# An attention-then-experts kernel: the hand-written order of all engines renewed, and the last branch laid out anew with prefetch hints

## The chip, the cores and the metric

The kernel runs on one core of one Trainium2 chip. The metric is device microseconds of one execution, and the median over several runs. The core's engines are named as in the profile: PE is TensorE (matmuls), PEld its weight loads, DVE is VectorE, ACT is ScalarE, POOL is GpSimd and SP is SyncE. A "q" behind a name (PEldq, SPq) means the instructions that the engine's sequencer handles itself: waits, branches, register loads, DMA issues.

## The reference, cut to what matters

An attention with 32 memory slots per head runs first; its output, 4608 tokens of 512 numbers, goes through a dense pair of matrices and through one of eight experts, chosen per token:

```python
a = softmax(phi, axis=2)                      # over the sequence
k_m = einsum('bhsm,bhsd->bhmd', a, k); v_m = einsum('bhsm,bhsd->bhmd', a, v)
attn_out = softmax(q @ k_m.T / sqrt(64)) @ v_m                 # 8 batches, 8 heads, 576 x 64
x = attn_out.transpose(0, 2, 1, 3).reshape(4608, 512)
y = maximum(x @ w1_dense, 0) @ w2_dense
e = argmax(x @ w_gate, axis=1); g = softmax(x @ w_gate)[e]
y += g * (maximum(x @ w1[e], 0) @ w2[e])                       # per token its own expert
```

## The kernel before

The eight batches are worked one after the other, overlapped by about a batch. For batch b the steps are, in the order of their data: loads `Lphi`, `Lk`, `Lv`, `Lq`; the exponential of phi (`e0`, `e1`, ACT); its column sums (`z`) and the sums with k and v (`kv`, both PE); scaling (`rz`, `kvm`, DVE); turning (`T`, PE) and copying (`kTc`, `vTc`); turning q (`qT0`, `qT1`, DVE); scores (`s`, PE), exponential (`ET0`, `ET1`, ACT), sums (`Z0`, `Z1`, PE), logarithm and inverse (`ln`, `inv`, ACT), the product `A0`, `A1` (DVE). The values are not multiplied out: they are folded into the first matrix of each expert (`fd` dense, `fe` chosen expert; PE), copied (`vd`, `ve`), and the hidden rows are made from A (`hd0..3`, `he0..3`, PE, each 8 matmuls), made non-negative (`Hd`, `He`, ACT or DVE) and multiplied by the second matrix (`yd0..4`, `ye0..4`, PE, each 4 matmuls of 128x512, the last of 64 rows). `Yd` writes the dense part of the output tile `y` (ACT or DVE), `Ye` adds the expert's part (DVE).

One expert is guessed for a whole batch (`choose`, DVE, from the mean value; `wv` reads the number into a POOL register) and its two matrices are loaded (`w1`, `w2`, POOL's queue), or copied from an earlier batch's slot (`cw1`, `cw2`, DVE). For each token `gates` finds the true expert. `pn` (PE) and `flags` (DVE, five small instructions) count the tokens whose expert was another. If there are any, a block with the slow way (`others`, one body per batch, 8 bodies of some 950 PE instructions) runs; with this data there are none, and every engine but SP reads the count from memory, branches past the block and goes to the closing barrier.

The order of everything is written out by hand: the table `ORDER` names each step with its batch and, after a slash, its engine (A for ACT, V for DVE, P for POOL) or, for `warm`, the number of dummy matmuls. Each engine executes its own steps in that order. Loads of q, k, v and the matrices are issued by POOL, the stores `o0`, `o1` (512 KB each) and `o4` (two of 64 KB) by SP, each queue in the order of the table.

Three things around the change are needed below. The output tile `y` has four buffers (`NKEEP`), so the fifth batch's first `Yd` waits until all stores of one earlier batch have landed, and which batch that is follows from the order of the stores. The dense and the expert part of a row share three accumulators of PSUM (the pool `one`), so a `Yd` that waits keeps an accumulator. And the last batch (7) folds its gate into the hidden rows, so that its `Yd` step stands behind `ye`.

## Time and profile before

| | us |
|---|---|
| median of 3 runs | 169.8 (169.19 to 170.12) |
| the profiled execution | 169.38 |
| its span, first to last instruction | 167.7 |
| TensorE busy | 149.8 (89% of the span) |
| VectorE busy | 119.9 (72%) |
| ScalarE busy | 94.0 (56%) |
[...]

The profile's times count from the span's first instruction. 169.38 less 167.7 leaves 1.68 us outside the span. "Idle before" and "waits" name the instruction that waited, how long its engine stood still, and who ended the wait.

### The profile page before, as it was taken

The numbers are of one execution on the slowest core, as the hardware profiler recorded it, in microseconds if no ns is written. First come the engines' busy times: TensorE is split into PE (matmuls) and PEld (weight loads), VectorE is DVE, ScalarE is ACT, GpSimd is POOL, SyncE is SP. The second block draws the span as 40 slices with busy tenths as digits, with TensorE's granted clock in tenths as the row PEclk, the third lists the DMA queues.
The fourth block names the chain that finished last, engine by engine and source line by source line (L and its number), as shares of the span: only waits on it lengthen the run. The fifth ranks groups of instructions, "written<-read, shape, count | busy, mean of one in ns | idle before, by whom it ended". The sixth has DMA issues, their size and how long they took to land.

```text
span 167.7 us, 4923 instructions
## 1 busy us (share of the span) xinstructions
PE 149.8 (89%) x2011; PEld 83.5 (50%) x2011; DVE 119.9 (72%) x354; ACT 94.0 (56%) x190; POOL 33.8 (20%) x56
## 2 busy tenths in 40 slices
PE   7969999999988999999999977699999999999900
PEld 2334455455555664565465633354554765655300
DVE  0524566787997999999598861979788997985110
ACT  3200564695539758964996388228289979630210
POOL 7810251009000750090002002940000000000000
PEclk9999999999999999999999999999999999999995
DMA  5999999999999999999999998999999299831460
GB/s 138 152 203 228 257 211 213 210 257 232 210 260 230 214 265 212 206 254 234 211 225 245 162 277 350 138 192 208 279 207 212 66 349 381 306 119 58 156 260 8
DMA packets 20500, 36.04 MB, mean 215 GB/s; under 512 B 1268, under 2 KB 14580, under 8 KB 20472
## 3 DMA queue, kind: packets, MB, share of 16 engines
q0 software_dynamic: 16336, 25.63, 79.7%
q1 hardware_dynamic: 4056, 9.98, 16.2%
q8 instruction: 17, 0.28, 0.6%
q14 instruction: 11, 0.09, 0.2%
q10 hardware_dynamic: 80, 0.07, 0.2%
HBM read 51.92 MB, written 9.44 MB: 366 GB/s over the span
## 4 chain that ended last, share of the span: by engine, by line
PE 39%; DMA 31%; DVE 14%; issue 5%; ACT 3%; POOL 1%; POOLq 1%; SPq 1%; DVEq 1%; ACTq 0%
PE p_y L788 20%; DMA kv<-in_v_dram 16%; PE p_h L712 10%; DMA W<-in_moe_w_dram 8%; DMA out_dram<-y 6%; DVE y L830 3%; PE p_kv L370 2%; PE p_vw L693 2%; DVE W L606 2%; PE p_x L320 1%; PE p_s L454 1%; ACT ET L467 1%; DVE qT L438 1%; DVE A L515 1%; POOLq L585 1%
## 5 line engine op out<-in xcount | busy, mean ns | idle before, releaser
L788 PE MATMUL p_y<-w2d,HTd 128*128 128x512 f16 (+1 forms) x192 | 37.3, 346 | 2.6 <-DVE y L823 2.3
L788 PE MATMUL p_y<-W,HTe 128*128 128x512 f16 (+1 forms) x192 | 36.0, 346 | 0.4 <-ACT y L821 0.4
L752 ACT ACTIVATE HTd<-p_h 128x576 f16<-128x576 f32 x27 | 16.8, 650 | 18.4 <-PE p_h L712 18.3
L830 DVE SCALAR_TENSOR_TENSOR y<-p_y,gm,y 128x512 f32<-128x512 f32 (+1 forms) x35 | 23.6, 692 | 3.9 <-PE p_y L788 2.2
L788 PEld LDWEIGHTS <-HTd 128*128 128x128 f16 (+1 forms) x192 | 14.6, 101 | 15.7 <-issue 4.8
L788 PEld LDWEIGHTS <-HTe 128*128 128x128 f16 (+1 forms) x192 | 14.8, 101 | 15.3 <-issue 4.1
L240 POOL DMA_DIRECT2D W<-in_moe_w_dram x8 | 4.6, 570 | 87.5 <-DMA W<-in_moe_w_dram 30.5
L821 ACT ACTIVATE y<-p_y 128x512 f32<-128x512 f32 (+1 forms) x25 | 14.0, 567 | 12.4 <-PE p_y L788 12.3
L320 PE MATMUL p_x<-onesb 128*128 128x512 f16 x68 | 19.0, 422 | 1.2 <-DVE ones L258 1.2
L712 PE MATMUL p_h<-A,vwd 128*128 128x288 f16 x128 | 19.6, 286 | 0.3 <-DVE A L515 0.2
L712 PE MATMUL p_h<-A,vwe 128*128 128x288 f16 x128 | 19.2, 286 | 0.0
L467 ACT ACTIVATE ET<-p_s 128x512 f16<-128x512 f32 x16 | 9.7, 604 | 12.6 <-PE p_s L454 12.6
L823 DVE TENSOR_SCALAR y<-p_y 128x512 f32<-128x512 f32 (+1 forms) x15 | 9.3, 632 | 8.3 <-PE p_y L788 4.5
L752 ACT ACTIVATE HTe<-p_h 128x576 f16<-128x576 f32 x21 | 13.2, 659 | 3.5 <-PE p_h L712 3.5
L332 ACT ACTIVATE E<-phi 128x576 f16<-128x576 f32 x16 | 10.6, 681 | 7.6 <-DMA phi<-in_phi_dram 7.6
L712 PEld LDWEIGHTS <-vwd 128*128 128x128 f16 x128 | 11.7, 97 | 6.2 <-issue 1.6
L712 PEld LDWEIGHTS <-vwe 128*128 128x128 f16 x128 | 11.8, 98 | 5.7 <-issue 0.8
L392 DVE TENSOR_SCALAR kvm<-p_kv,rz 128x64 f16<-128x64 f32 (+1 forms) x32 | 8.0, 310 | 6.0 <-PE p_kv L370 5.7
L515 DVE TENSOR_TENSOR A<-ET,lnz 128x576 f16<-128x576 f16 x16 | 11.5, 750 | 1.1 <-ACT lnz L508 1.0
L438 DVE STREAM_TRANSPOSE qT<-q 128x512 f32<-128x512 f32 x16 | 11.0, 691 | 0.2 <-DMA q<-in_q_dram 0.2
L320 PEld LDWEIGHTS <-onesb 128*128 128x128 f16 x68 | 6.6, 106 | 9.2 <-issue 3.4
L508 ACT ACTIVATE lnz<-lnz 128x576 f32<-128x576 f32 x16 | 10.7, 690 | 0.2
(95 smaller groups left out, 195.9 us busy)
## 6 DMA issues: line engine op xcount, KB each, us to landing
W<-in_moe_w_dram POOLq DMA_DIRECT2D x16, 512.0 KB, 8.6
out_dram<-y SPq DMA_DIRECT2D x16, 512.0 KB, 5.2
kv<-in_v_dram POOLq DMA_DIRECT2D x8, 576.0 KB, 17.6
kv<-in_k_dram POOLq DMA_DIRECT2D x8, 576.0 KB, 15.7
q<-in_q_dram POOLq DMA_DIRECT2D x8, 576.0 KB, 15.5
phi<-in_phi_dram POOLq DMA_DIRECT2D x7, 576.0 KB, 16.4
out_dram<-y SPq DMA_DIRECT2D x15, 64.0 KB, 4.9
phi<-in_phi_dram SPq DMA_DIRECT2D x2, 288.0 KB, 4.2
```

The costliest lines, as they stand in the source:

```text
L320: nc.tensor.matmul(p_x, lhsT=onesb, rhs=onesb[:, 0:1].to_broadcast([128, 512]), start=True, stop=True)
L332: nc.scalar.activation(out=x["E"][:, :, hs].rearrange("p t j m -> p j t m"), in_=x["phi"][:, hs], func=AF.Exp,)
L438: nc.vector.transpose(out=o[:, :, 0 : 2 * KQ], in_=i[:, 0:n].rearrange("p (h t) d -> p h t d", h=NP))
L467: nc.scalar.activation(out=ET.rearrange("m (h c) -> m h c", h=2)[:, :, 0:256].rearrange("m h (p k) -> m h p k", k=KQ), in_=p_s[:, :, 0:256 ...
L508: nc.scalar.activation(out=lnz, in_=lnz, func=AF.Exp, scale=-1.0)
L515: eng.tensor_mul(out=st[b]["A"][:, a], in0=st[b]["ET"][:, a, 0:S], in1=st[b]["lnz"][:, a])
L712: nc.tensor.matmul(p_h[:, h, 0:HC], lhsT=vw[:, g, 128 * ft : 128 * ft + 128], rhs=a[:, g, HC * h : HC * h + HC], start=(g == 0), stop=(g = ...
L752: nc.scalar.activation(out=o, in_=in_[:, :, 0:HC], func=AF.Relu)
L788: nc.tensor.matmul(p_y[n * u : n * u + n, to : to + w], lhsT=HT[:, ft, at], rhs=w2[:, ft, w * u : w * u + w], start=(first and ft == 0), s ...
L821: nc.scalar.activation(out=o, in_=p_y, func=AF.Copy, scale=1.0 / SC)
L823: nc.vector.tensor_scalar(out=o, in0=p_y, scalar1=1.0 / SC, scalar2=None, op0=ALU.mult)
L830: nc.vector.scalar_tensor_tensor(out=o, in0=p_y, scalar=x["gm"][:, c : c + 1], in1=o, op0=ALU.mult, op1=ALU.add)
```

## The change

The table `ORDER` is replaced by another one with the same steps (66 dummy matmuls in place of 68, the step `nap` gone, a step `hint` new; some copies go to ACT in place of DVE and the other way round). The planner that writes such a table now has the waits for output buffers in its model. The last branch gets a label, its block is laid out right behind the branch instruction (it falls through into the block when the count is not zero, and jumps when it is zero), and a prefetch hint for this branch is put on PE, DVE, ACT and POOL.

```diff
 ORDER = """
-Lphi1:0 cones:0 Lwg:0 cid:0 warm:0/4 Lphi0:0 Lv:0 warm:0/4 Lk:0 Lq:0 e0:0 Lw1d:0 warm:0/4 e1:0 Lphi:1/P
+Lphi0:0 cones:0 Lwg:0 Lv:0 cblk:0 warm:0/4 Lphi1:0 cid:0 warm:0/4 Lk:0 e0:0 Lq:0 e1:0 Lphi:1/P warm:0/1
...
-ye4:7 ye3:7 Yd4:7/V o4:7/A yd1:7 Yd3:7/A yd0:7 o0:6 ye1:7 ye0:7 Yd1:7/V ye2:7 Yd0:7/A o0:7 pn:0 Yd2:7/A
-flags:0 o1:7 nap:7
+he2:7 He1:7/V yd2:7 He2:7/A ye4:7 ye3:7 Yd4:7/A o4:7/A yd1:7 Yd3:7/A yd0:7 o0:0 ye1:7 ye0:7 Yd1:7/A pn:0
+ye2:7 Yd0:7/A flags:0 o0:7 Yd2:7/V o1:7
...
+    @step("hint")
+    def _(b, i, e):
+        tc.mark_branch_hint_location("fix", engines=(ENG.PE, ENG.DVE, ENG.Activation, ENG.Pool))
...
-    with tc.If(anyv > 0, preferred_fallthrough_block=False):
+    with tc.If(anyv > 0, preferred_fallthrough_block=True, label="fix"):
```

**The stores of batches 1 to 3.** SP's queue, from the first store on. Before, y_1486, y_1011 and y_1939 are the tiles of batches 2, 1 and 3 (L847 is half an `o4`, L836 an `o0` or `o1`):

```order
L847 DMA out_0_dram<-y_1486 32x2x256 x2
L847 DMA out_0_dram<-y_1011 32x2x256 x2
L836 DMA out_0_dram<-y_1939 32x4x1024
L847 DMA out_0_dram<-y_1939 32x2x256 x2
L836 DMA out_0_dram<-y_1486 32x4x1024
L836 DMA out_0_dram<-y_1939 32x4x1024
L836 DMA out_0_dram<-y_1486 32x4x1024
```

Of the change, the same place on SP; y_1485, y_1004 and y_1946 are the tiles of batches 2, 1 and 3:

```order
L847 DMA out_0_dram<-y_1485 32x2x256 x2
L847 DMA out_0_dram<-y_1004 32x2x256 x2
L847 DMA out_0_dram<-y_1946 32x2x256 x2
L836 DMA out_0_dram<-y_1485 32x4x1024 x2
L836 DMA out_0_dram<-y_1946 32x4x1024 x2
```

Before, batch 3 was the first whose four stores were all issued, its last one (`o1:3`) standing behind one of batch 2; the tile of batch 4 takes its buffer. Of the change batch 2 is first, with both large stores ahead of those of batch 3, and batch 4 takes that buffer.

**The end of the main part.** PE's last instructions before the branch. Before, p_y_3383 is the accumulator of the last output rows, p_n the count:

```order
L788 LDWEIGHTS HTe_3364
L788 MATMUL p_y_3383<-W2_86,HTe_3364 128x512
L858 LDWEIGHTS onesb_123
L858 MATMUL p_n_3432<-own_120,onesb_123 1x48
L851 LDWEIGHTS ones8_122
L851 MATMUL p_y_3383<-ones8_122 2x2
L976 TENSOR_LOAD any_i_128
L976 ISA x2
L977 COMPARE_AND_BRANCH
L977 UNCONDITIONAL_BRANCH
L979 TENSOR_LOAD fl_i_127
```

Of the change, the same place on PE; p_y_3389 is the accumulator of the last rows:

```order
L862 LDWEIGHTS onesb_123
L862 MATMUL p_n_3432<-own_120,onesb_123 1x48
L788 LDWEIGHTS HTe_3369
L788 MATMUL p_y_3389<-W2_86,HTe_3369 128x512
...
L788 LDWEIGHTS HTe_3369
L788 MATMUL p_y_3389<-W2_86,HTe_3369 128x512
L980 TENSOR_LOAD any_i_128
L980 ISA x2
L981 COMPARE_AND_BRANCH
L983 TENSOR_LOAD fl_i_127
```

The count moves ahead of the last four matmuls of 128x512, `nap` (L851 before) is gone, and behind the branch there stands no jump any more but the block itself; the few instructions of the way past it now stand behind the eight bodies, next to the closing barrier.

**The start of POOL.** The difference on POOL's queue from its first instruction (const and ident are constants, kv a batch's k and v):

```order
-L1007 UNCONDITIONAL_BRANCH
+L1011 UNCONDITIONAL_BRANCH
+L1011 BRANCH_PREFETCH_HINT
+L210 DMA kv8_138<-in_v_dram 128x4x576
 masks.py:197 MEMSET ident128_121 128x128
 masks.py:199 ISA
 masks.py:199 AFFINE_SELECT ident128_121<-ident128_121 128x128
-L210 DMA kv8_148<-in_v_dram 128x4x576
```

The first load moves ahead of the making of the identity matrix. The hint, though `hint` stands near the table's end, is the first instruction of the main part here, and so it is on PE, DVE and ACT.

## Rows read from the trace of the kernel before

**Rows 1.** The page: span, and busy tenths of PE and DMA in 40 slices

```profile
span 167.7 us, 4923 instructions
...
PE   7969999999988999999999977699999999999900
...
DMA  5999999999999999999999998999999299831460
```

**Rows 2.** Busy time by stretch: start:end, length, then each engine's busy time

```profile
1.20:33.70 32.50, 30.14 (x454) 14.58 (x454) 17.07 (x63) 11.62 (x25) 11.26 (x17) 1.00 1.10 209
33.70:159.40 125.70, 119.40 (x1556) 68.94 (x1557) 101.96 (x285) 81.48 (x165) 22.05 (x34) 1.00 0.98 224
```

**Rows 3.** Waits of PE: line and releaser, us in total, times, longest

```profile
PE p_y L788 <- DVE y L823: 2.3, 1, 2.3
...
PE p_att L617 <- DVE A L515: 0.4, 1, 0.4
```

**Rows 4.** Chain that ended last, 88 to 112 us: start, length, what

```profile
92.70 0.80 PE p_kv L370 x72
...
94.10 0.86 PE p_y L788 x4
...
97.92 0.41 PE p_vw L693 x7
...
99.36 5.64 DMA out_dram<-y
```

**Rows 5.** Timeline of SP, 94 to 101 us: start, length, instruction, count

```profile
97.40 3.36 SPq L836 DMA_DIRECT2D out_dram<-y  x3
```

**Rows 6.** Stores and writers of the tile y, 95 to 125 us: landing times

```profile
DMA to landing us min/median/max: 5.6/6.3/6.7
```

**Rows 7.** Timeline of all engines, 158 to 161 us

```profile
157.67 0.69 DVE L823 TENSOR_SCALAR y<-p_y 128x512 f32<-128x512 f32 x1 [3.37 <-PE p_y L788]
...
159.40 0.60 ACT L821 ACTIVATE y<-p_y 128x512 f32<-128x512 f32 x1 [0.27 <-PE p_y L788]
159.51 0.20 DVE L873 TENSOR_REDUCE flags<-p_n 1x8 f32<-1x48 f32 x1 [1.15 <-PE p_n L858]
...
160.12 0.14 DVE L881 CAST any_i<-fl_any 1x1 int32<-1x1 f32 x1
```

**Rows 8.** Lines L977 and L1007: ns min/median/max, first and last start

```profile
L977 PEldq COMPARE_BRANCH  x2: 89/1956/3822, 161.8 to 162.3; - x2
...
L1007 POOLq EVENT_SEMAPHORE  x4: 17/17/17, 166.9 to 167.6; - x4
L1007 SPq DRAIN  x3: 7/7/7, 164.3 to 167.2; - x3
L1007 POOLq DRAIN  x3: 46/106/1278, 165.6 to 167.4; - x3
...
L1007 PEldq DRAIN  x2: 8/40/73, 166.1 to 167.2; - x2
```

**Rows 9.** The last store alone (L836, issued at 160.0): its landing

```profile
DMA to landing us min/median/max: 3.9/3.9/3.9
```

**Rows 10.** DMA queues, 160.5 to 167.7 us: packets, MB, share

```profile
q8 instruction: 2, 0.03, 2.1%
q14 instruction: 5, 0.04, 1.9%
```

**Rows 11.** Timeline of POOL, 0.8 to 3 us

```profile
1.62 0.88 POOL L210 DMA_DIRECT2D kv<-in_v_dram  x1 [0.18 <-issue]
```

**Rows 12.** Timeline of PE's weight loads, 28 to 34 us

```profile
31.20 1.41 PEld L788 LDWEIGHTS <-HTd 128*128 128x128 f16 x8 [0.55 <-DMA w2d<-in_moe_w_dense_dram]
...
33.73 0.11 PEld L693 LDWEIGHTS <-vT 64*32 64x32 f16 x8 [0.39 <-DMA W<-in_moe_w_dram]
```

**Rows 13.** The load of phi issued at 22.0 us (L193): its landing

```profile
DMA to landing us min/median/max: 18.5/18.5/18.5
```

**Rows 14.** The page: queues over the whole span, packets, MB, share

```profile
q8 instruction: 17, 0.28, 0.6%
```

## The prediction

> **What bounds the kernel now.** I read the page first: PE's row of tenths is full from the fourth slice on, and so is the DMA row for 28 slices of 4.19 us, up to about 117 us [rows 1]. Two things are close to their limit at once, so I need to know which one sets the pace where. The busy times by stretch say it for PE [rows 2]: from 33.70 to 159.40 us it works 119.40 of 125.70 us. All that a new order can win there is the remaining 6.3 us. Ahead of that it has little real work, since the inputs are still on their way: the first weights of an expert's matrix are loaded at 33.73, as soon as that matrix has landed, after 0.39 us of waiting, and the dense matrix held PE's loads up by 0.55 us at 31.20 just before [rows 12]. So the start is a DMA stream, the middle is PE, and the end, 159.4 to 167.7, is neither.

> The list of PE's waits then shows that one wait makes up the largest part of the 6.3 us: 2.3 us in the dense output rows, released by DVE's copy of such rows, and 0.4 us right behind it for A [rows 3]. The chain of waits names what DVE itself waited for: a store of 5.64 us from 99.36 on [rows 4]. It is the third kind of thing in this kernel, an output buffer: the y tile of batch 4 takes over the buffer of batch 3, whose last store is the second of three that SP issues from 97.40 on [rows 5].

> The end: the last accumulator is done at 159.4, ACT copies it from 159.40 to 160.0, and the last store is issued at 160.0 [rows 7, 9]. The count's matmul `pn` stands behind all others on PE, and the count itself takes DVE from 159.51 to 160.26 [rows 7]. Then every engine branches. PE's second branch instruction, the jump past the bodies, lasts 3.822 us from 162.3, and PE's drain comes only at 166.1; POOL's drain begins at 165.6 and takes 1.278 us; SP, which has hardly any code, drains at 164.3, when the last store has landed (160.0 and 3.9) [rows 8, 9]. In this stretch two blocks of 16 KB come in over PE's instruction queue and five pieces over the other one [rows 10]. So the closing barrier waits for engines that fetch code, not for the data: POOL is the last at 166.9, and 0.8 us later the program ends [rows 8].

> **The change part by part.** I sum against the profiled execution, 169.38 us (span 167.7, 1.68 outside); the median of the runs is 0.42 above it.

> The output buffer. Of the change batch 4 takes batch 2's buffer, and both large stores of batch 2 stand at once behind the half stores of batch 3. Batch 2's rows are long complete, so the only thing in front of them on SP are those two half stores, which need batch 3's last rows. In the new table these rows' matmuls stand three times four matmuls of 0.86 us [rows 4], a `z` and an `hd` ahead of the sums `kv:5`: an estimate of 3.9 us. Less 1.5 us until DVE has added the rows, and less three issues of 0.6 us, SP issues `o1:2` about 0.6 us ahead of `kv:5`. The stores around there land after 5.6 to 6.7 us [rows 6], so 5.0 to 6.1 us behind `kv:5`. Needed is it when the first `yd:4` is done. Before, from `kv:5` (92.70) to `fe:4` (97.92) it is 5.2 us [rows 4]; the new table has one `ye` of 0.86 less in between, and then 0.41 and 0.86 for `fe:4` and `yd3:4`: 5.6 us. So the 2.3 and 0.4 us shrink to between nothing and half a microsecond. I take **-2.5 us**, with bounds of 0 (the wait stays as long) and -2.7.

> The count ahead of the last rows. `pn` ends 0.86 us ahead of the last matmul in place of behind it, so DVE's five instructions run beside the last matmuls, and all engines read the count about 0.8 us earlier. The last copy moves from ACT (0.60 us [rows 7]) to DVE, behind the count, where such a copy takes 0.69 us [rows 7], and the 0.1 us of `pn` is now in front of it: the last store starts about 0.2 us later. That store is what the earlier branch must not be confused with: nothing on SP moves earlier.

> The branch. Before, the way past the block stood in line and the jump from it to the closing barrier was the far one. Of the change the compare instruction itself jumps far, to the way out, which lies next to the barrier. The number of far jumps on the path stays one; what can save time is the hint alone. If it brings the target in before the jump is made, PE, DVE and POOL come to the barrier soon after the branch that started at 162.3 before and starts at 161.5 now; POOL's 1.278 us of drain end before 164, and the end is set by the last store: SP's first drain at 164.3 before, 0.2 later now, 0.8 for the barrier and an estimated 0.1 until SP's signal is seen, so 165.4 in place of 167.7: **-2.3 us**. If it does nothing, the branch is 0.8 us earlier and so is the end: -0.8. Cover for the fetches that remain: the store, 3.9 us long, which also caps the gain.

> [...] The PE row shows 3.822 us for a jump and two 16 KB blocks of code on its queue. [...]

> The start. The first load leaves POOL after the identity matrix, at 1.62 [rows 11]; now it leaves ahead of it, at most 0.6 us earlier, less a hint instruction. Ten loads stand in front of the matrix that PE waits for at 33.73, and the queue is full, so an earlier start can shift all of it; but loads on SP's queue share the engines in these first microseconds. I take **-0.3** (bounds 0 and -0.6). Two dummy matmuls less cost or save nothing, they fill waiting time.

> POOL's queue otherwise: one load of k and v (`Lv:2`) now stands behind the wait for the second batch's expert. A load issued at 22.0 lands only 18.5 us later [rows 13], so the queue has work until after 40 us and the later issue is hidden; if it weren't, the price is one load's turn, some 2.7 us by the spacing of landings (31.2, 33.73 [rows 12]).

> All else in the table: the sums of PE's work ahead of each `kv` and `fe` are the same to within one step of 0.86 us, so PE's order is nearly kept. Copies change sides between ACT and DVE, 0.60 against 0.69 us each. New small waits cannot be read from the trace of before; bounds are 0 and 2.3 us (as long as the longest of PE in the middle [rows 3]). I take **+0.4**, the size of the lesser one, since the work is so alike.

> Sum: -2.5 - 2.3 - 0.3 + 0.4 = -4.7. 169.38 less 4.7 is 164.7; on the median's level 165.1 us.

> **The rivals.**
> 1. The forecast: both the buffer wait and the far jump go. 165.1, own range 163.6 to 166.2. For it: both are single, large, and named by the trace. Chance 0.48.
> 2. The hint does nothing (it is the first instruction of the main part on each engine, and nearly all blocks that PE's queue brings, 17 over the span [rows 14], come between it and the branch). Then -2.5 - 0.8 - 0.3 + 0.4 = -3.2: 166.6. [...] Chance 0.20.
> 3. The hint works, but the middle keeps its waits: the store of batch 2 lands late, or a wait of 2.3 us takes its place. -2.3 - 0.3 + 0.4: 167.6. Against it: the new store is one with its data ready. Chance 0.14.
> 4. Neither: -0.8 and -0.3 with 0.4: 169.1, no change that can be told. Chance 0.09.
> 5. [...] Chance 0.09, with what else may be slower in a new table.

> **How the numbers follow.** A measurement of this kernel tells about 0.5% from no change: 168.95 to 170.65. Cases 1 and 2 are faster, and most of 3: 0.80. Case 4 and the rest of 3: 0.11. Case 5: 0.09. The time is case 1's, 165.1. The range takes in cases 1 to 3 with their bounds: down to 163.2 (start -0.6, no new waits, wait wholly gone), up to 168.4 (case 3 with its new waits a little larger); left out are most of case 4 and case 5.

> **What would show it.** In the profile of the changed kernel: DVE's wait for a store ahead of its copy at L823 and PE's 2.3 us behind it gone; PE busy above 121 of the same 125.7 us behind the first expert's matrix; the PE branch at the end well under 1 us, the drains of PE, DVE and POOL ahead of SP's, and the last store's landing as what the barrier waits for. Wrong it would be if the branch still lasts 3.8 us, if the code blocks on PE's queue still arrive after the branch, if the y tile of batch 4 still waits, or if PE's idle time in the middle is as much as before under other names.

## The result, and the profile after

The median of the changed kernel is 168.62 us (166.07 to 169.92, 20 runs), that of the kernel before in the same comparison 169.9 us (168.23 to 170.85, 20 runs); the ratio is 0.989, 95% interval 0.985 to 0.993. The change makes the kernel 1.1% faster. Forecast were 165.1 us, range 163.2 to 168.4: the time lies above the range, and of the 4.7 us expected 1.3 came. Ratios here leave disturbed runs out, medians hold all runs. The profiled execution took 169.25 us (before: 169.38), so these two traces have to show where a gain of more than 4 us was lost.

The page of the changed kernel first: span, busy times, and the tenths of PE and DMA.

```profile
span 167.5 us, 4921 instructions
...
PE 152.3 (91%) x2008; PEld 82.1 (49%) x2008; DVE 117.3 (70%) x351; ACT 96.0 (57%) x193; POOL 34.1 (20%) x56
...
PE   6599999999998899999999999999979999999930
...
DMA  4999999999999999999999799999999689546451
```

The holes of PE's row in the middle [rows 1] are smaller, and one digit of its empty end is filled. Its start is thinner. Busy times by stretch, cut at the same events as [rows 2] (first dummy; first weights of an expert's matrix, `fe:0`; end of the last matmul of the y rows):

```profile
1.27:36.72 35.45, 32.50 (x454) 14.16 (x454) 15.09 (x61) 13.13 (x27) 11.11 (x17) 1.00 1.10 218
36.72:160.41 123.69, 119.81 (x1557) 67.91 (x1556) 101.39 (x288) 82.51 (x167) 22.80 (x35) 1.00 0.99 220
```

The middle went from 125.70 to 123.69 us: -2.0. The end, 160.41 to 167.5, takes 7.1 us, where [rows 2, 1] leave 8.3: -1.2. And the start, which the prediction had at -0.3, is **3.0 us longer**: `fe:0` begins at 36.72, not 33.73. That is the sum: +3.0 - 2.0 - 1.2 = -0.2, the 0.2 us between the two spans. (The table of the runs below cuts at the last y matmul's own end, 159.36 before, so that its stretches differ from these by up to 0.1 us.)

**The start.** PE's timeline in the changed kernel (start, length, instruction, what it waited for):

```profile
1.27 4.02 PE L320 MATMUL p_x<-onesb 128*128 128x512 f16 x9 [1.27 <-DVE ones L258]
7.31 0.40 PE L343 MATMUL p_att<-ones,E 128*128 128x2 f16 x9 [2.02 <-ACT E L332]
7.58 1.01 PE L320 MATMUL p_x<-onesb 128*128 128x512 f16 x2
8.52 0.58 PE L299 MATMUL p_w<-ident,wgt 4*64 4x4 f16 x16
9.04 4.87 PE L320 MATMUL p_x<-onesb 128*128 128x512 f16 x11
13.84 0.76 PE L370 MATMUL p_kv<-kv,E 64*32 64x64 f16 x72
```

and the same place in the kernel before:

```profile
1.19 7.11 PE L320 MATMUL p_x<-onesb 128*128 128x512 f16 x21 [1.19 <-DVE ones L258]
8.22 0.41 PE L299 MATMUL p_w<-ident,wgt 4*64 4x4 f16 x16
8.57 0.38 PE L343 MATMUL p_att<-ones,E 128*128 128x2 f16 x9
10.55 0.75 PE L370 MATMUL p_kv<-kv,E 64*32 64x64 f16 x72 [1.60 <-DMA kv<-in_v_dram]
```

L320 are the dummy matmuls (`warm`). Before, 21 stand in a row, fill the wait for the inputs and end 2.3 us ahead of the first sum with v (L370), which waits for v. The new table puts `z:0` (L343) behind the first nine. It needs E, which comes at 7.31, so PE stands still for 2.02 us. Eleven more dummies stand between the transposes of the gate weights (L299) and that sum (L370), and they take 4.87 us: 0.44 each, twice the 0.2 us of the later ones before (ten in the 2.0 us from 6.2 to 8.2). The 21 of before take 0.34 on average: up to 5.86 us the weight loads of the dummies start 0.43 us apart there, and only the last ten take 0.2. No wait is shown in front of L370 any more: v is there (a load on POOL that waits for the same v goes out at 9.76), and dummies stand in its way. The list of PE's waits has the same item on top, and of [rows 3] what is left of the output buffer, 0.2 us:

```profile
PE p_att L343 <- ACT E L332: 2.0, 1, 2.0
...
PE p_y L788 <- DVE y L823: 0.2, 1, 0.2
```

At `fe:0` itself PE no longer waits for the expert's matrix [rows 12]. Its load goes out when the expert has been chosen, and the choice hangs on L370: issued at 22.70 instead of 19.97, it lands 10.2 us later, at 32.9, and PE comes to it only at 36.72.

```profile
22.70 0.74 POOL L240 DMA_DIRECT2D W<-in_moe_w_dram  x1 [12.38 <-issue]
```

```profile
DMA to landing us min/median/max: 10.2/10.2/10.2
```

The granted clock reads 1.00 in all these stretches, also from 9.10 to 13.80 us, where dummies take 0.44 us. It doesn't show the difference here; the dummies' own duration does.

**The middle.** DVE's first copy into the tile of batch 4, before and in the changed kernel, and of the changed kernel the landing of `o1:2`, issued at 97.3:

```profile
105.22 0.69 DVE L823 TENSOR_SCALAR y<-p_y 128x512 f32<-128x512 f32 x1 [3.73 <-DMA out_dram<-y]
```

```profile
105.86 0.69 DVE L823 TENSOR_SCALAR y<-p_y 128x512 f32<-128x512 f32 x1 [2.35 <-PE p_h L712]
```

```profile
DMA to landing us min/median/max: 8.4/8.4/8.4
```

DVE still stands idle for 2.35 us. The line names PE, but the copy begins 0.2 us after the store has landed (97.3 and 8.4), and in e2, e8 and e14, with the same order of stores, the same copy waits 4.0, 3.5 and 2.5 us for the store by name. So the buffer still comes late; what changed is that PE loses only 0.2 us by it.

**The end.** The lines of branch and barrier, to be held against [rows 8]:

```profile
L981 PEldq COMPARE_BRANCH  x1: 414/414/414, 161.2 to 161.2; - x1
...
L1011 POOLq DRAIN  x3: 50/97/1212, 162.1 to 167.2; - x3
L1011 SPq DRAIN  x3: 7/7/7, 166.6 to 166.9; - x3
...
L1011 PEldq DRAIN  x2: 8/8/8, 161.9 to 167.0; - x2
```

PE's branch lasts 0.414 us instead of 3.822; PE drains at 161.9, POOL from 162.1 for 1.2 us, and SP is last at 166.6, as foretold. But the last store, issued at 161.2, takes longer than the 3.9 us of [rows 9]:

```profile
DMA to landing us min/median/max: 5.1/5.1/5.1
```

DMA in 40 slices of the 7 us behind the last matmul, for the changed kernel,

```profile
DMA  0000799999998999687402121111010000000000
...
q8 instruction: 1, 0.02, 1.3%
q14 instruction: 3, 0.02, 0.9%
```

and for the kernel before:

```profile
DMA  0000049999999999999981600000000000000003
```

Before, both last stores are sent at full width and are over after 3.9 us. In the changed kernel the row breaks from the 17th slice on, 2.8 us behind the last matmul, while the last store is under way, and then trickles at one or two tenths for some 2 us: of the 16 DMA engines that is the share of two or three, an estimate from these digits. Four fetches of code (16 KB for PE, three of 8 KB) come in during that stretch: they begin at 162.7, when 0.44 MB of the last two stores are still to be sent. Before, the first fetch behind the branch begins at 163.0, and 0.00 MB (11 packets) is left.

### The profile page after: what moved, and what is told of

Same layout as the page of the kernel before. It is cut to its first block, busy times and chain, and to the rows that moved or that the text cites. A ratio compares the mean times of both kernels' runs of the same rounds, so it can differ in the third digit from the quotient of the medians.

```text
span 167.5 us, 4921 instructions
## 1 busy us (share of the span) xinstructions
PE 152.3 (91%) x2008; PEld 82.1 (49%) x2008; DVE 117.3 (70%) x351; ACT 96.0 (57%) x193; POOL 34.1 (20%) x56
## 4 chain that ended last, share of the span: by engine, by line
PE 64%; DVE 14%; DMA 9%; ACT 4%; issue 3%; POOLq 1%; SPq 1%; DVEq 0%
PE p_y L788 28%; PE p_h L712 16%; PE p_x L320 7%; DMA W<-in_moe_w_dram 5%; DVE y L830 4%; PE p_kv L370 3%; DVE kvm L392 3%; DMA phi<-in_phi_dram 3%; PE p_s L454 2%; DMA out_dram<-y 2%; PE p_vw L693 2%; ACT ET L467 2%; PE p_z L486 1%; PE p_att L617 1%; PE p_att L397 1%
## 5 line engine op out<-in xcount | busy, mean ns | idle before, releaser
L788 PE MATMUL p_y<-W,HTe 128*128 128x512 f16 (+1 forms) x192 | 36.7, 346 | 0.2 <-DVE y L830 0.2
L752 ACT ACTIVATE HTd<-p_h 128x576 f16<-128x576 f32 x29 | 18.5, 648 | 16.6 <-PE p_h L712 16.3
L320 PE MATMUL p_x<-onesb 128*128 128x512 f16 x66 | 21.6, 463 | 1.4 <-DVE ones L258 1.3
L752 ACT ACTIVATE HTe<-p_h 128x576 f16<-128x576 f32 x20 | 12.6, 653 | 5.4 <-PE p_y L788 3.7
L712 PEld LDWEIGHTS <-vwd 128*128 128x128 f16 x128 | 11.2, 97 | 5.2 <-issue 0.6
L823 DVE TENSOR_SCALAR y<-p_y 128x512 f32<-128x512 f32 (+1 forms) x15 | 9.1, 613 | 5.8 <-PE p_y L788 3.2
L320 PEld LDWEIGHTS <-onesb 128*128 128x128 f16 x66 | 6.5, 111 | 9.6 <-issue 5.5
L606 DVE COPY W<-W 128x2048 f16 x14 | 9.7, 694 | 2.0 <-DMA W<-in_moe_w_dram 2.0
```

The source lines that it names most:

```text
L320: nc.tensor.matmul(p_x, lhsT=onesb, rhs=onesb[:, 0:1].to_broadcast([128, 512]), start=True, stop=True)
L606: nc.vector.tensor_copy(out=W[:, b].rearrange("p t f -> p (t f)"), in_=W[:, 0 : b + 1][:, ds(st[b]["slot"], 1)].rearrange("p o t f -> p (o ...
L712: nc.tensor.matmul(p_h[:, h, 0:HC], lhsT=vw[:, g, 128 * ft : 128 * ft + 128], rhs=a[:, g, HC * h : HC * h + HC], start=(g == 0), stop=(g = ...
L752: nc.scalar.activation(out=o, in_=in_[:, :, 0:HC], func=AF.Relu)
L788: nc.tensor.matmul(p_y[n * u : n * u + n, to : to + w], lhsT=HT[:, ft, at], rhs=w2[:, ft, w * u : w * u + w], start=(first and ft == 0), s ...
```

## The experiments

One table for all runs. "Before" is the median of the kernel before, run together with it; start is the time of `fe:0`, middle the time from there to the end of the last y matmul, end from there to the end of the span, all from the run's profile.

| run | median, us (runs) | before | ratio (95%) | start | middle | end |
|---|---|---|---|---|---|---|
| before | 169.9 (20) | | | 33.73 | 125.6 | 8.4 |
| changed | 168.62 (20) | 169.9 | 0.989 (0.985-0.993) | 36.72 | 123.7 | 7.1 |
| e1 dummies together | 165.97 (6) | 170.41 | 0.983 (0.974-0.991) | 32.90 | 124.1 | 6.9 |
| e2 eleven out | 166.33 (6) | 170.41 | 0.985 (0.978-0.993) | 33.99 | 124.1 | 6.9 |
| e7 before, new start | 173.61 (6) | 170.41 | 1.023 (1.014-1.033) | 37.16 | 126.7 | 9.1 |
| e4 before, branch | 169.5 (12) | 170.41 | 0.997 (0.993-1.001) | 34.03 | 126.8 | 8.3 |
| e3 no hint | 169.77 (12) | 169.94 | 0.997 (0.992-1.001) | 37.89 | 122.3 | 7.5 |
| e5 e4, 8 instructions less | 167.85 (6) | 169.94 | 0.988 (0.982-0.994) | 32.76 | 126.7 | 6.2 |
| e6 before, stores | 168.68 (6) | 169.94 | 0.989 (0.981-0.997) | 32.70 | 124.5 | 8.6 |
| e8 e1, halves | 164.22 (6) | 169.94 | 0.966 (0.961-0.971) | 33.46 | 123.9 | 4.8 |
| e9 gap bridged | 166.85 (4) | 169.45 | 0.985 (0.980-0.990) | 36.26 | 122.4 | 7.3 |
| e10 halves only | 167.17 (6) | 169.45 | 0.986 (0.981-0.992) | 37.41 | 122.9 | 5.1 |
| e11 two terms | 167.16 (6) | 169.45 | 0.988 (0.982-0.995) | 32.41 | 124.1 | 6.2 |
| e12 e1, count last | 163.99 (6) | 169.45 | 0.967 (0.962-0.972) | 33.31 | 124.3 | 6.2 |
| e13 two terms, swapped | 166.32 (6) | 170.65 | - | 35.16 | 123.8 | 6.2 |
| e14 twenty ahead | 168.6 (1) | 170.65 | - | 36.21 | 123.7 | 7.0 |
| e15 e12, halves | 163.61 (6) | 170.65 | 0.961 (0.955-0.967) | 33.25 | 123.0 | 5.0 |

### The start: order of the dummies, or order of the loads?

**e1**: the changed kernel, its dummies in one row.

```
-wgt:0/V z:0 Lw1d:0 warm:0/2 Lk:1 wgm:0 warm:0/4 wgc:0 ciota:0 Lv:1 rz:0 warm:0/4 Lq:1 warm:0/2 warm:0/1
-vv:0 Lw2d:0
+wgt:0/V Lw1d:0 warm:0/2 Lk:1 warm:0/4 ciota:0 Lv:1 warm:0/4 Lq:1 warm:0/2
+wgm:0 z:0 wgc:0 rz:0 vv:0 Lw2d:0
```

> The changed kernel, with 21 dummy matmuls in one stretch ahead of the gate transposes and the sums over E, as the kernel before has them (one dummy fewer, all else as changed). Order theory: the 3.0 us that fe:0 begins later are those of the dummies, which stood apart, with TensorE idle for 2.0 us between them, and ran at 0.43 us each instead of 0.22. Then the first values' sum (L370) begins at 10 to 11 us instead of 13.84, fe:0 at 33.5 to 34.5 instead of 36.72, and the time falls by 2 to 3 us, to 165.6 to 166.6. Load theory: the new order of the loads sets the start (the second w1 leaves at 22.7 instead of 20.0). Then L370 may begin earlier, but fe:0 stays above 36 and the time within 0.5 us of 168.6.

PE's timeline of e1:

```profile
1.28 7.65 PE L320 MATMUL p_x<-onesb 128*128 128x512 f16 x21 [1.28 <-DVE ones L258]
...
9.51 0.75 PE L370 MATMUL p_kv<-kv,E 64*32 64x64 f16 x72
```

L370 begins at 9.51, `fe:0` at 32.90 (even earlier than expected), and the median is 4.4 us below the kernel before, where the change alone had 1.3. The ratios, 0.983 and 0.989, are nearer to each other and their intervals overlap; the clear pair is e8 and e10 below, which differ by this row of dummies alone: 0.966 against 0.986. The loads are in the changed order here, so the load theory falls.

**e2**: the eleven dummies between `wgm:0` and `vv:0` left out, `z:0` where the change puts it.

> The changed kernel without the 13 dummies... 11 of them left out: none stands between the gate transposes and the first values' sum. Order theory with the dummies as mere filler: L370 begins when v has landed (about 9.8 us) and fe:0 about 3 us earlier than 36.72, time 165.6 to 166.6. Order theory with the engine's speed as the cause: the dummies are gone, but the real matmuls that follow run at the lower speed for some time (L370's stretch of 72 takes well over 0.76 us, the next dummies 0.43 each), so that fe:0 gains 1 to 2.5 us only, 166.2 to 167.6. Load theory: fe:0 stays above 36, time 168.1 to 169.1.

L370 begins at 9.71, as soon as v is there (0.72 us of waiting), `fe:0` at 33.99. So most of the loss is the dummies standing in the queue. The remaining 1.1 us against e1 would fit the speed (the two dummies behind L370 take 1.04 us, in e1 0.61), but it isn't shown: with the order of before, unchanged up to L370, `fe:0` lies between 32.41 (e11) and 35.16 (e13).

**e7**: the kernel before with the changed kernel's start.

> The kernel before with the changed kernel's start alone (its loads, dummies, sums over E and gate transposes up to the first values' sum), all else as before. Order theory: L370 begins near 13.8 instead of 10.55, fe:0 2.5 to 3.5 us later than 33.73, time 172.4 to 173.4 against 169.9. Load theory, with the rest of the order to blame: fe:0 within 0.7 us of 33.7 and the time within 0.7 us of 169.9.

L370 begins at 14.75 and `fe:0` at 37.16; the median is 3.2 us above the kernel before. The start costs as much in the one order as in the other.

**e9**: five dummies more in front of `z:0`.

```
+warm:0/4 warm:0/1 wgt:0/V z:0
```

> The changed kernel with five dummy matmuls more in front of its first sums over E (z:0), where TensorE stood idle for 2.0 us; all else stays, the eleven behind the gate transposes too. Gap theory (the dummies behind ran at 0.43 us because the engine had been idle): without the gap they take 0.22 us each, the first values' sum begins at 11.0 to 12.0 us instead of 13.84, in spite of five dummies more. Rival (the sums over E and the transposes, with few columns, are what keeps the speed down, or the speed comes at a time of its own): the eleven stay at 0.4 us or more and the values' sum begins at 13.5 us or later. Apart from that, ten instructions of TensorE are added ahead of the branch (4042 in place of 4032): by the place theory its branch takes 3.8 to 4.8 us again in spite of the hint, and the end then costs 0.5 to 1.5 us more; if place has nothing to do with it, it stays at 0.41 us.

```profile
1.27 5.42 PE L320 MATMUL p_x<-onesb 128*128 128x512 f16 x14 [1.27 <-DVE ones L258]
8.14 0.38 PE L343 MATMUL p_att<-ones,E 128*128 128x2 f16 x9 [1.44 <-ACT E L332]
...
9.25 4.21 PE L320 MATMUL p_x<-onesb 128*128 128x512 f16 x11
```

Missed: E came later in this execution, PE still stood idle for 1.44 us, and the eleven took 0.38 each. It doesn't tell the theories apart. (Its branch is told of below.)

**e14**: eleven more in front, the eleven behind stay, eleven later ones go.

> The changed kernel with twenty dummies instead of nine in a row in front of its first sums over E (z:0); the two and the eleven behind stay, and eleven later ones are left out, so that TensorE's code is as long as before. Row theory (the dummies behind ran at 0.43 us because the row in front of them was cut short at 5.3 us and the engine then stood idle): the eleven take 0.22 us each and the first values' sum begins at 11.3 to 12.3 us instead of 13.84. Rival (the sums over E and the transposes between them slow whatever follows): they stay at 0.4 us or more and the values' sum begins at 13.5 us or later.

```profile
1.27 6.14 PE L320 MATMUL p_x<-onesb 128*128 128x512 f16 x20 [1.27 <-DVE ones L258]
7.84 0.38 PE L343 MATMUL p_att<-ones,E 128*128 128x2 f16 x9 [0.42 <-ACT E L332]
...
8.95 2.56 PE L320 MATMUL p_x<-onesb 128*128 128x512 f16 x11
11.44 0.75 PE L370 MATMUL p_kv<-kv,E 64*32 64x64 f16 x72
```

The eleven take 0.23 us each, and L370 begins at 11.44: the row theory holds, the sums and transposes in between do no harm. `fe:0` gains little (36.21), probably since the eleven dummies left out later are missed there: PE then waits 2.11 us for A, and the stretch behind that wait has a mean granted clock of 0.64, where the same column reads 1.00 from 12 to 24 us:

```profile
24.00:28.00 4.00, 3.35 (x33) 0.64 1.11 216
```

### The branch: what the hint does, and when

**e3**: the changed kernel without the step `hint`.

> The changed kernel without the hint step; the branch's new layout stays. Hint theory: TensorE's branch takes 3.8 to 4.8 us instead of 0.41, its drain comes at 165.2 or later, the last store is no longer the last to arrive and the kernel is 0.8 to 1.6 us slower than the changed one (ratio to before 0.993 to 1.0 where the changed kernel had 0.989). Layout theory (the hint does nothing, the block behind the branch helps): the branch stays at 0.41 us and the ratio at 0.989.

```profile
L981 PEldq COMPARE_BRANCH  x1: 4586/4586/4586, 161.0 to 161.0; - x1
```

The hint it is, not the layout: 4.586 us against 0.414. The median goes up by 1.1 us against the changed kernel, each taken with its own kernel before (0.2 below it here, 1.3 there). In the profiles the end grows by only 0.4 us (7.5 against 7.1), because the last store lands late here too, 5.3 us after its issue.

**e4**: the kernel before with hint and new layout alone. **e5**: the same with four dummies fewer.

```
+    @step("hint")
+    def _(b, i, e):
+        tc.mark_branch_hint_location("fix", engines=(ENG.PE, ENG.DVE, ENG.Activation, ENG.Pool))
...
-    with tc.If(anyv > 0, preferred_fallthrough_block=False):
+    with tc.If(anyv > 0, preferred_fallthrough_block=True, label="fix"):
...
-vd0:0/V w1:0 warm:0/4 ln1:0     (e5 alone)
+vd0:0/V w1:0 ln1:0
```

> The kernel before with the hint and the branch's new layout alone. Forecast of the prediction: TensorE's branch instruction takes 0.1 to 0.5 us instead of 3.82 and the last store's landing (160.0 plus 3.9) sets the end: 2.3 us less, 167.6. Second theory, from the changed kernel's trace: the code that is fetched then meets the last store, which lands 1.2 us later (5.1 us after its issue): 1.0 to 1.3 us less, 168.6 to 168.9. Third, the hint does nothing: 0.8 us less, 169.1. Fourth, the layout does harm: the time stays or grows.

> The kernel before with the hint and the new layout, as in the run before of these two alone, where TensorE's branch still took 4.37 us, and with four dummy matmuls fewer (behind w1:0), which are eight instructions of TensorE. Place theory: in that run the branch stood at the very end of a 16 KB block of TensorE's code (4039 instructions in the trace ahead of it, 4032 in the changed kernel), so that the hint came too late; eight instructions earlier it takes 0.3 to 0.6 us, the last store's landing sets the end, and the kernel is 1.8 to 2.6 us faster than before (ratio 0.984 to 0.990). Other theory: what keeps the hint from working lies elsewhere in the order of before (the hint is lost under the loads, or the count comes too late for it); then the branch stays at 4 us or more and the ratio at 0.995 to 1.0.

PE's branch in e4, and then in e5 and in e9:

```profile
L981 PEldq COMPARE_BRANCH  x1: 4366/4366/4366, 163.3 to 163.3; - x1
```

```profile
L981 PEldq COMPARE_BRANCH  x1: 414/414/414, 162.0 to 162.0; - x1
```

```profile
L981 PEldq COMPARE_BRANCH  x1: 4606/4606/4606, 159.4 to 159.4; - x1
```

In e4 the hint works on DVE and POOL (their next instruction starts 0.6 and 0.5 us after the branch does, in e3 4.2 and 4.4; on ACT it is 0.5 in both) and fails on PE (4.366 us); the end stays at 8.3 us and the time within what can be told. What decides here is where the branch stands in PE's code. The pages count 2011 matmuls and as many weight loads in e4, 2013 in e9, and the hint fails; with 2008 (changed, e10, e14), 2007 (e1, e5, e8, e11 to e13, e15) and 1997 (e2) it works. Eight instructions fewer repair e4, ten more break the changed kernel. PE's code queue brings 16 blocks of 16 KB over the span in every run where it works, and 17 or 18 in the others (before, e3, e4, e6, e7, e9). In the kernel before one of them comes in between 163.0 and 163.6, inside the branch of 3.822 us from 162.3. Whether the border is the end of such a block was not shown.

In e5 the end takes 6.2 us, 2.1 less than before: nearly the prediction's -2.3, where only the branch is changed (and four dummies).

### The end: why the last store takes longer

**e8**: e1, with the last batch's two stores of 512 KB as four of 256 KB, each behind its own rows. **e10**: the same on the changed kernel.

```
-... yd0:7 o0:0 ye1:7 ye0:7 Yd1:7/A pn:0 ye2:7 Yd0:7/A flags:0 o0:7 Yd2:7/V o1:7
+... yd0:7 o0:0 p3:7 ye1:7 ye0:7 Yd1:7/A p1:7 pn:0 ye2:7 Yd0:7/A flags:0 p0:7 Yd2:7/V p2:7
```

> The changed kernel with the 21 dummies together (as in the run of that) and, in addition, the last batch's two stores of 512 KB made four of 256 KB, each sent as soon as its rows are done, so that only 256 KB are left to send behind the last copy. Collision theory (the last store took 4.9 to 5.1 us instead of 3.9 because the code that all engines fetch behind the branch shares DMA engines with the rest of its data): the data are out earlier, the last store lands 3.0 to 4.0 us after its issue, and the kernel is 0.8 to 1.9 us faster than the one with the dummies together. Rival (the landing itself is slower, whatever the size, or pieces of 2 KB cost more): within 0.5 us of it, or slower.

> The changed kernel with the last batch's two stores made four of 256 KB as in the run before, its dummies as the change has them. Collision theory: from the end of the last matmul to the end of the span 4.7 to 5.3 us in place of 7.08, and the time 1.8 to 2.4 us below the changed kernel's (ratio to before 0.973 to 0.979), with fe:0 still at 36.5 or later. Rival (most of the 2 us of that run came from the start): the stretch at the end stays above 6.3 us and the ratio at 0.985 or more.

In e8 the end takes 4.8 us where e1 had 6.9, and the last piece lands 3.0 us after its issue:

```profile
DMA to landing us min/median/max: 2.4/2.4/3.0
```

In e10 the end is 5.1 us, as expected, with the start as late as in the change (37.41). Its median is 2.3 us below the kernel before, only 1.0 more than the change; the ratio expected was missed, and why the 2.0 us of the end do not all show is open. Against e8 it has the dummies of the change and nothing else different: 2.0% of the time, or some 3 us, is the price of their order.

**e12**: e1 with the count, and the last copy on ACT, where the kernel before has them.

```
-Yd1:7/A pn:0 ye2:7 Yd0:7/A flags:0 o0:7 Yd2:7/V o1:7
+Yd1:7/A ye2:7 Yd0:7/A o0:7 pn:0 Yd2:7/A flags:0 o1:7
```

> The changed kernel with the 21 dummies together, and with the count (pn, flags) and the last copy (on ScalarE) put back where the kernel before has them, behind the last matmuls. Collision theory: moving the count ahead brought the branch, and the code fetched behind it, into the time in which the last store's data are sent; put back, the fetch begins 0.7 to 0.9 us later against the store's issue, the last store lands 3.9 to 4.4 us after its issue instead of 4.9, and from the last matmul to the end of the span it takes 6.0 to 6.5 us instead of 6.85. Rival (the landing has another cause): it stays at 4.8 to 5.1 us and the stretch at 6.8 us or more.

The landing of its last store, and DMA in the 7 us behind the last matmul:

```profile
DMA to landing us min/median/max: 4.3/4.3/4.3
```

```profile
DMA  0000079999999999999846100000000000000000
```

The trickle of the changed kernel is gone and the end takes 6.2 us; of the 0.7 us against e1, 0.6 are in the landing (4.9 there). What is left of the stores when the fetches come in shows why: the DMA of 0.6 us from the first fetch on, of the changed kernel (162.6 to 163.2) and of e12 (161.3 to 161.9), packets, MB, share:

```profile
q1 hardware_dynamic: 55, 0.20, 99.4%
```

```profile
q1 hardware_dynamic: 4, 0.00, 0.3%
```

The same four fetches meet a store at full width in the one and nothing in the other. With e8 this shows the collision from both sides: less data behind the branch, or a later branch, and the last store lands early again. All runs whose last store is one of 512 KB agree: with the count ahead it lands after 4.9 to 5.3 us (changed, e1, e2, e3, e9, e14), with the count last after 3.9 to 4.5 (before, e4 to e7, e11 to e13), with the hint and without.

**e15**: e12 and the halves.

> The changed kernel with all three repairs: the 21 dummies together, the count behind the last matmuls as before, and the last batch's stores in four pieces of 256 KB. If each repair takes away its own part of the collision, from the last matmul to the end of the span it takes 4.7 to 5.2 us instead of 6.18 and the time is 162.3 to 163.5 (ratio 0.957 to 0.963). Rival: GpSimd's drain, which begins after the branch and takes 1.2 us, then ends last; 5.3 us or more, and no faster than the runs with one repair of the end (ratio 0.965 to 0.967).

The end takes 5.0 us, as expected and no less than in e8, and the rival's mechanism is there: the last piece lands at 159.3, but POOL's drain, behind the later branch, ends 1.2 us after 159.3.

```profile
L1018 POOLq DRAIN  x3: 50/97/1212, 159.3 to 161.0; - x3
L1018 SPq DRAIN  x3: 7/7/7, 159.9 to 160.7; - x3
```

The median, 163.61 us, lies just above the range given. This is the lowest ratio, 0.961, though its interval overlaps those of e8 and e12; all three beat both kernels.

### The middle: the output buffer alone, and the sum of two terms

**e6**: the kernel before with `o0:2 o1:2` ahead of `o0:3`, in SP's order only.

> The kernel before with SP's stores of the third batch (o0:2, o1:2) in front of the fourth batch's, as the changed kernel has them; nothing else. Forecast of the prediction: VectorE's wait for its output buffer near 104 us and TensorE's 2.3 us behind it are gone, 2.0 to 2.6 us faster than before (ratio 0.985 to 0.988). Rival: the wait moves on to another store or to VectorE's queue; less than 0.8 us faster (ratio above 0.995).

```profile
PE p_kv L370 <- DMA kv<-in_v_dram: 2.2, 1, 2.2
```

The wait for the buffer is gone, on DVE too, and a new one of 2.2 us stands 10 us ahead of its place; the middle is 1.1 us shorter than before. (One of its six executions took 491.78 us; why is not known, and the median hardly sees it.) In e6 the two stores leave at 81.4 and 82.0, land 7.7 to 9.2 us after, and share the DMA engines with the load of v that PE then waits for (from 80 to 98 us the loads' queue moves 3.23 MB, before 3.47; the queue of the stores 1.43, before 0.26); the changed kernel sends them 15 us later, from 96.6 on. The order was right, the place was mine and wrong.

**e11**: e5 and e6 together. **e13**: e5, with `o0:2` and `o0:3` only changing places, so that the store leaves near 95 us.

> The kernel before with the two terms of the prediction that runs have shown by themselves, and nothing else of the change: the third batch's stores ahead of the fourth's, and the hint with the new layout (with four dummies fewer, as in that run). If the two terms add up and only the start's order took the gain away: 4.0 to 4.9 us faster than before, 165.0 to 166.0 (ratio 0.971 to 0.977). If they get in each other's way (the wait that goes is taken up at the end, or the end waits for something else): 1.5 to 3 us, ratio 0.982 to 0.991.

> The kernel before with the two larger terms of the prediction: the hint and the new layout (with four dummies fewer), and the third batch's first store ahead of the fourth's, by a swap of the two on SP's queue, so that it leaves near 95 us as in the changed kernel and not at 81 us. If the wait of the run before was the stores' early place: no wait for the load of v near 92 us, none for the output buffer, from fe:0 to the last matmul 123 to 124.5 us, from there to the end 6.2 us, and 3.8 to 4.9 us faster than before (ratio 0.971 to 0.978). Rival (TensorE loses the same time elsewhere as soon as one wait goes): fe:0 to the last matmul 125 us or more, ratio 0.983 or more.

e11 has the same misplaced stores and the same wait (2.0 us); its runs lie between 164.54 and 168.65 and settle nothing. In e13 the middle takes 123.8 us (126.7 in e5, from which it differs by the swap alone) and the end 6.2, both as expected, and the median is 4.3 us below the kernel before (166.32 against 170.65, from runs that spread by 3.6 us). The two waits that were to be gone are only smaller: PE still waits 0.8 us for v, and DVE 2.0 us for the output buffer, without PE behind it. What held PE for another 1.0 us, ahead of 102.06, the record doesn't show.

## Why the prediction was wrong

**The step that failed is "The start".** It read: "I take -0.3 (bounds 0 and -0.6). Two dummy matmuls less cost or save nothing, they fill waiting time." It counted the dummies and looked at POOL's first load, but not at where the dummies stand on PE's queue. The first load left 0.1 us earlier (1.50 instead of 1.62) and v was there by 9.76 instead of 10.55, but PE did not use it: +3.0 us in the profiled pair, in e7 3.2 us on the median. A dummy fills waiting time only if it is through before the data that PE waits for arrive. Eleven of them stood behind a wait for E, at 0.44 us each instead of 0.2, ahead of work whose data had landed. With that "the start is a DMA stream" no longer held: the expert's matrix was there 3.8 us before PE came to it. Over the runs with the late start (changed, e3, e9, e10, e14) `fe:0` begins at 36.9 us on average, over those with the same rest and an early start (e1, e2, e8, e12, e15) at 33.4; the last matmul ends at 159.9 and 157.3. So 3.5 us are lost in the start, and 0.9 of them are made good in the middle: 2.6 us net.

**The output buffer** (-2.5, and +0.4 for new waits): right in size, and partly by luck. DVE's copies no longer hold up PE there (2.3 us before, 0.2 after), and the middle is 2.0 us shorter in the profiled pair, forecast 2.1. But the store was to land 5.0 to 6.1 us behind `kv:5`; it left 0.1 us ahead of `kv:5` (97.36) instead of 0.6, took 8.4 us instead of 5.6 to 6.7, and landed 8.3 us behind it. So "the y tile of batch 4 still waits", which the prediction named as a sign of being wrong, is what DVE shows. That PE loses so little, 0.2 us here and 0.9 at most (e2), was not in the working; the new table puts more of PE's other work between the first rows that need the buffer, but no run tests that by itself. A single profile is uncertain by about 1 us here: four profiles with the old middle (before, e4, e5, e7) have 125.6 to 126.8, ten with the new one 122.3 to 124.3.

**The branch** (-2.3): right where the branch is changed alone (e5, -2.1), -1.2 in the changed kernel. The sentence that failed is "Cover for the fetches that remain: the store, 3.9 us long". The store does cover the fetches, and the fetches lengthen the store, to 5.1 us. They do so because of an edit that I had costed at an earlier branch only, "The count ahead of the last rows": it takes the branch, and what is fetched behind it, into the middle of the last store (put back in e12, the end is 0.7 us shorter). The hint is not the cause, for without it the store lands as late (e3, 5.3 us).

**The rivals.** Rival 2 (the hint does nothing, since nearly all blocks come between it and the branch) falls with e3: 0.414 us against 4.586. (With the branch a few instructions further on, in e4 and e9, the rival came true on PE: 4.366 and 4.606 us.) Rival 5 (slower) did not come: the ratio is 0.989. Rival 3 (the store of batch 2 lands late, or a wait comes in place of the one removed) came true in its first half, without its price: the store is late, PE is not. A new wait came in e6 and e11, where the stores had another place, not in the change.

**The sum.** Without the start the two large terms do come: e13 is 4.3 us below the kernel before, forecast for these two were 4.8. That rests on medians of runs that spread by 3.6 us; in the profiles the middle and the end of e13 are together 3.9 us shorter than before. Three slips of the working decided nothing: the bounds named for the low end of the range add up to 164.2, not 163.2; DMA's row is full for 30 slices, up to 130 us; and 31.2 to 33.73 is 2.5 us, not 2.7.

## What to carry to other kernels

Filler work belongs to the order as much as real work: for each piece read what stands behind it in its queue, and when that could run; a filler behind a wait can cost both its place and its speed (here 0.44 us a dummy instead of 0.2). When a wait goes from the list of the engine that bounds, look whether it is gone or has only been hidden. What is "covered" by a transfer may share its engines with it (here the last store took 5.1 us instead of 3.9), so ask of both what happens to the other. And a gain that hangs on where an instruction falls in the code (here three matmuls and their weight loads: PE's branch takes 0.414 us in the changed kernel with 2008, 4.366 in e4 with 2011) should be looked up in the trace after every edit.
